# Linear attention into a routed MLP on one core: freeing the first half batches from a shared PSUM buffer, splitting one cast, and turning 512 tokens ahead of 64

## The chip, the cores and the metric

The kernel runs on one core of a Trainium2 chip. The metric is device time in microseconds of one execution, from the first to the last instruction of the program; the figure given is the median of several executions. The kernel before takes 963.41 us (median of three, 963.19 to 964.06). The profile of it is of one further execution whose recorded span is 960.4 us; all positions in time below are counted from the start of that span.

## The reference

For 8 batches and 8 heads, with 576 tokens of 64 channels each, the attention part computes with phi(x) = elu(x) + 1

```python
kv  = einsum('bhsd,bhse->bhde', phi(k), v)      # k^T v
z   = sum(phi(k), axis=2)
num = einsum('bhsd,bhde->bhse', phi(q), kv)
den = einsum('bhsd,bhd->bhs', phi(q), z)[..., None] + 1e-06
x   = (num / den)  -> transposed and reshaped to (4608, 512)
```

Then comes a mixture of 8 experts over all tokens: logits = x @ w_gate, P = exp(logits) brought to balance by eight rounds of row and column scaling, and out = sum over e of P[:, e] * (relu(x @ w1[e]) @ w2[e]), with w1[e] of 512 x 1024 and w2[e] of 1024 x 512. All inputs are fp32 in device memory; the products are computed in fp16 with fp32 sums.

## The kernel before, in words

**A planner writes the order.** Every piece of work is handed to `add` (lines 33 to 46) with its engine or engines, an assumed duration, what it depends on, and the buffers that it takes (`acq`) and uses (`use`). `_Plan.run` (lines 52 to 119) plays this forward as a list scheduler: it takes the engine that can start earliest, among what can start then the task with the lowest `prio`, and emits its instructions. So the order of the instructions on each engine is fixed when the program is built. On the chip each engine goes through its list in that order, and an instruction that waits holds up all behind it on its engine. After all tasks are added, a long string `ranks` (lines 1026 to 1163) overwrites the `prio` of tasks by their number and, with a suffix `act` or `dve`, nails a task that either engine could do to one of them. The tasks of the front and of expert 0 are in it; the tensor engine's order for experts 1 to 7 is written out by hand as a chain (lines 1011 to 1024).

**The front: 16 half batches.** `att(b, g)` (line 246) handles four heads of one batch, n = 2b + g counting the half batches from 0 to 15. It loads k, q and v (line 269; for n of 0, 1 and from 6 on by SyncE, for 2 to 5 by GpSimd), computes exp on ScalarE (line 285), and phi on VectorE in two steps (lines 298 and 301). The fp32 v is cast to fp16 into `vv` (line 315), which keeps a column of ones beside each head, so that k^T v and the sums z come from one set of 18 matmuls (line 330) into `kv_ps`, a PSUM tile [128, 2, 512] of which columns 0 to 129 of each of its two banks are used; it has one buffer. A multiplication then masks this into `kvz` (lines 341 and 343). phi(q) is transposed on TensorE (line 358) and copied out (line 362) as `qpT`. The denominators are ten small matmuls (line 373) into `den_ps`, 20 columns wide; VectorE adds 1e-6 and takes the reciprocal (lines 379 and 381, `rden`). The numerators come in three groups, of two, two and one row tile (line 397), and VectorE multiplies each with `rden` into `xn` (line 402). The five row tiles start at token pairs js = 0, 2, 4, 6 and 7, in units of 64 tokens: the last overlaps the fourth, so that tiles 0 to 3 hold tokens 0 to 511 and only the last 64 tokens come from tile 4. Each channel chunk of 128 is then transposed with five transposes (line 413) and copied with one copy of 576 columns (line 417) into `xT`, which holds all tokens channels first.

**Shared PSUM.** The tag `att` has two buffers (`aps`, line 159). Transposed q, the denominators, the numerators, the transposed x, the logits and later pieces of the experts all take one of the two in the order of the plan (pool `p_att`). For n = 0 the first two numerator groups use `ye0` and `ye1` instead (`ps_home`, line 250).

**What follows.** `layer1(0, g)` (line 560) multiplies 512 tokens with w1 of expert 0 in eight column tiles f. For g = 0 the first four are cut in two: channel chunks 0 and 1 (half batch 0 alone) first, then chunks 2 and 3, which need half batch 1 (lines 572 and 573). It waits for `xt_done` of all batches that its tokens lie in: g = 0 lies in batch 0 alone, g = 1 in batches 0 and 1. The second layer (line 809) follows in `unit_plain`, in groups of four matmuls over half of w2 each, with two PSUM buffers `ye0` and `ye1`, and an accumulator takes both halves. `x_blocks` (line 598) prepares and stores shuffled sums of `xT`, `logits` (line 425) multiplies with w_gate, and `sinkhorn` does the eight rounds. Experts 1 to 7 follow, with a form of multiplication that saves one product in eight.

**Loads at the start.** SyncE issues k, q, v of n = 0 and 1 at once. On GpSimd's queue come, in an order that the dependencies fix: w1 of expert 0 in two parts (after v of n = 0 has landed, line 522), the loads of n = 2, those of n = 3, w2 of expert 0 in two parts (line 527), and then n = 4 and 5. `kqin` and `vin` have two buffers each, so the loads of n + 2 wait until those of n are read.

**Warm-up.** 34 tasks of one or two dummy matmuls (lines 503 to 513, 47 matmuls in all) with the lowest priority are spread over the first 18 us, to keep TensorE in work until the real matmuls come.

Of the kernel before, what the change touches and what calls it, by code (L numbers as in the profile page):

```python
# [122 lines left out]
def kernel(  # L123
# [45 lines left out]
    NX = 5  # L169
    MG = 99  # L170
# [67 lines left out]
    gates = {}  # L238
    v_land, kv_id = [], []
# [6 lines left out]
    def att(b, g):  # L246
# [67 lines left out]
        def f_v(e):  # L314
            copy(e, gvv["tile"][:, :, :, 0:D], gin["v"]["tile"])
        tvv.append(fadd({"act": 1.15, "dve": 0.76}, f_v, deps=[ta, tin["v"]],
                        use=[gvv, gin["v"]], prio=pr))
# [49 lines left out]
        gden, grd, gxn = S_.grp(p_att), S_.grp(p_rden), S_.grp(p_xn)  # L367

        def f_den(_):
            gden["tile"] = aps.tile([P, 5, 2, 2], FP32, tag="att", name="den_ps")  # L370
            for i, j in enumerate(js):
                for hh in range(2):
                    nc.tensor.matmul(gden["tile"][:, i, :, hh],  # L373
                                     lhsT=gq["tile"][:, hh, j:j + 2, :].rearrange("p j w -> p (j w)"),
                                     rhs=gz["tile"][:, hh, :, D], start=True, stop=True)

        def f_rd(_):
            grd["tile"] = fp.tile([P, 5, 4], FP32, tag="rden", name="rden")
            nc.vector.tensor_scalar(out=grd["tile"], in0=gden["tile"].rearrange("p i r h -> p i (r h)"),
                                    scalar1=1e-6, scalar2=None, op0=ALU.add)  # L380
            nc.vector.reciprocal(grd["tile"], grd["tile"])
        tden = fadd(("pe", 0.26), f_den, deps=tq + tz, acq=[gden], use=[gq, gz], prio=pr)
# [6 lines left out]
        for i0, i1 in ((0, 2), (2, 4), (4, 5)):  # L389
# [16 lines left out]
            txn.append(fadd(("dve", 0.14 + 0.275 * (i1 - i0)), f_xn, deps=[t1, trd, txa], use=[gn, grd, gxn], prio=pr))  # L406
        for c2 in range(2):
            gx = S_.grp(p_att)

            def f_xt(_, c2=c2, gx=gx):  # L410
                gx["tile"] = aps.tile([P, S], FP16, tag="att", name="xt_ps")
                for i in range(5):
# [3 lines left out]
            def f_xc(e, c2=c2, gx=gx):  # L416
                copy(e, xT[:, 2 * g + c2, S * b:S * b + S], gx["tile"])
            t1 = fadd(("pe", 0.3), f_xt, deps=txn, acq=[gx], use=[gxn], prio=pr)
            xt_done[(b, 2 * g + c2)] = fadd({"act": 0.64, "dve": 0.46}, f_xc, deps=[t1], use=[gx], prio=pr)
# [5 lines left out]
    def logits(b2):  # L425
# [11 lines left out]
        t1 = lg_pe[b2] = add(("pe", 1.0), f_l, deps=[xt_done[(b, c)] for b in (2 * b2, 2 * b2 + 1) for c in range(NDT)],  # L437
# [74 lines left out]
    for i in range(34):  # L512
# [47 lines left out]
    def layer1(e, g):  # L560
        gw1, tw1, gw2, tw2 = w_t[e]
        bs = range(512 * g // S, (512 * g + 511) // S + 1)
        xd_ = [xt_done[(b, c)] for b in bs for c in range(NDT)]
# [34 lines left out]
    def x_blocks(g):  # L598
        bs = range(512 * g // S, (512 * g + 511) // S + 1)
        deps = [xt_done[(b, c)] for b in bs for c in range(NDT)]  # L600
# [420 lines left out]
    for tt in (3, 2, 1, 0):  # L1021
# [5 lines left out]
        0:-50.0024 36:8.7509 38:8.7566 40:-50.0207 42:-49.9982 43:8.7608 44:-50.0228 45:8.7578 46:-50.0192  # L1027
        47:-50.0138 49:8.7452:act 50:-49.9982 51:-50.0108 52:-50.0204:act 54:8.7572 55:-50.0216 56:8.7563
        57:-49.9985:act 58:-50.0222 59:-50.0213 61:-50.0117 62:-50.0036 63:-50.012 64:8.759 65:-50.0135
        66:-98.0291 67:-50.012 68:8.7602:dve 69:-49.9994 70:-50.0129:act 71:-50.015 73:-50.0144 75:-49.9886  # L1030
        77:-50.0129 78:-49.9988 79:-50.0186 80:8.7587 81:-50.0207 82:-50.0027 84:-50.0198 85:-49.9829
        86:-49.9985:act 88:-98.021 89:-50.015:act 90:-50.0201 91:8.7617:dve 92:-50.0195 93:-50.0219
        95:-50.0162 96:8.7575 97:-50.0201 98:-50.0186 99:8.7464 100:-98.0051 101:-50.0195 102:-50.0144:act
        103:-50.0141 104:-50.0198 106:8.7632 108:8.7575 110:-49.9844 112:-50.0216 114:-50.0006 116:8.7575
        117:-50.0132 118:-50.0006 119:-50.021 120:-50.0192 121:-49.9982 123:-50.0201:dve 124:-50.0159
        125:-50.0225:dve 127:-50.0138 128:-50.0105:dve 129:8.762 130:-50.0213 131:-98.0054 132:-50.0189
        134:-49.9787 135:-50.0207 136:-49.9859 137:-50.003 138:-50.0018 139:-50.0228 140:-50.0153
        141:-50.0093:dve 142:-49.9811 143:-50.0003:dve 144:-50.0156 146:-50.012 148:-50.0147 150:-50.0237
        151:-50.021 152:8.7593 153:-50.0204 154:-50.0192 155:-50.0156 157:-50.0003:act 158:-50.0159
        159:8.7368:dve 161:-50.0117 162:-50.0147:act 163:-50.0021 164:-50.0213 165:-50.0222 166:8.7443  # L1040
        168:-50.021 169:-50.0231 170:-50.0168 171:-50.0267 172:-50.0216 173:-50.0144 174:-50.0228
        175:-50.0228:dve 176:-50.0201 177:-49.9787:act 179:-50.0063 181:-50.006 183:-50.0144 184:-50.0189
        185:-50.0189 187:-50.0168 189:-50.0048 191:8.7584 192:-49.9802 193:-50.0225 194:-50.0255
        195:-50.0201 196:-50.0219 198:-50.0195 199:-50.0132 200:-50.0207:dve 202:-50.0249 203:-50.0144
        204:-50.0015 205:-50.0213:dve 206:-98.0237 207:-50.012 209:-50.0183 210:-50.0204 211:-50.0258
        212:-50.0288 213:-50.0189 214:-50.0237 215:-49.9808 216:-49.9856:act 217:-50.0219 218:-50.0117:dve
        219:8.7602 221:-50.0153 223:-49.9991 225:-50.0015 226:-50.0165 227:-50.0225 228:-50.0162
        229:-98.0078 230:-50.0165 232:-50.0087:dve 233:-98.0054 234:8.7512:dve 236:-50.0216 237:-98.0051:act
        238:-50.0246 239:-50.0165:dve 240:-50.0219 241:-98.0048 243:-50.027 244:-50.0195 245:-50.0135
        246:-50.0126 247:-50.0228 248:-50.0123 249:-50.0159 250:-50.018:act 251:-98.0228 252:-49.9826  # L1050
        253:-50.018 255:-50.0213 257:-50.018 259:-50.0162 260:-50.0231 261:-98.0063 262:-50.0282 263:-50.012
        264:-50.0003 266:-50.0117:dve 267:-50.0159 268:8.7464:act 270:-50.0195 271:8.7509:act 272:-98.0054
        273:-50.0168 274:-50.0162 275:-98.0246 277:-50.015 278:-50.0213 279:-50.0243 280:-50.0273
        281:-50.0174 282:-98.0231 283:-98.003 284:-50.0198:act 285:-98.0261 286:-50.0228:dve 287:-98.0048
        289:-49.9814 291:-49.9808 293:-50.0267 294:-49.9856 295:-50.0282 296:-50.0045 297:-50.0243
        298:8.7446 300:-49.9805 301:-50.0276 302:-50.0186:dve 304:-50.0204 305:-50.0123:act 306:-50.0132
        307:-98.006:act 308:-50.0207 309:-50.0219 311:-49.9784 312:-50.0192 313:-50.0189 314:-50.0123
        315:-50.021 316:-50.012 317:-49.9754 318:-50.0135 319:-50.0162 320:-49.9826:act 321:-50.0015
        322:-50.0249 323:-50.0126 325:-98.0048 327:-50.0198 329:-50.0108 330:-50.0174 331:8.7458 332:-49.985
        333:-50.0162 334:-50.0153 336:-50.0159:dve 337:-50.0171 338:-49.9793:dve 340:-98.0294 341:-98.033  # L1060
# [140 lines left out]
```

The softmax here doesn't subtract the row's maximum and nothing guards it: scores larger than these inputs give would overflow.

## Time and profile before

| what | value |
|---|---|
| time, median of 3 | 963.41 us (963.19 to 964.06) |
| span of the profiled execution | 960.4 us |
| TensorE matmul busy | 954.2 us, 8833 instructions |
| VectorE, ScalarE, GpSimd busy | 773.4, 572.4, 114.1 us |
| granted TensorE clock | 1.00 in all stretches |
| memory traffic | 121.99 MB by DMA, mean 127 GB/s, 270 to 345 GB/s in the first 120 us |

A page of the profile lists the busy time of each engine, then the span in 40 slices, the DMA queues, the chain of work that ended last, and the costliest groups of instructions. PE is the tensor engine's matmuls and PEld its weight loads, which overlap them. DVE is VectorE, ACT ScalarE, POOL GpSimd and SP SyncE. A group is named by its line in the kernel, and "out<-in" are the tiles' names. In an answer of the timeline the columns are the start, the duration and the engine; brackets at the end tell how long the engine sat idle before, and what ended that. Three things matter for reading it here: the dummy matmuls count as busy, an instruction of TensorE is shown with its latency and overlaps the next (four matmuls of 512 columns are listed with 1.03 us, but follow each other in 0.86), and the front, where the change lies, is the first 130 us.

### The profile page before, as it was taken

What the parts mean: (1) busy time and instruction counts of PE and PEld (TensorE: products, weight loads), DVE (VectorE), ACT (ScalarE), POOL (GpSimd) and SP (SyncE); (2) the same over time, 40 slices, a digit from 0 to 9 for tenths busy, and PEclk for the clock granted to TensorE, in tenths of its full rate; (3) what the DMA queues carried; (4) which work ended last, traced back from release to release, by engine and by line L of the source; (5) the groups of instructions that cost most, each with busy time, mean ns of one, the idle gap of its engine ahead of it and who ended that gap; (6) DMA issues with size and microseconds to landing.
All of it is one profiled execution on the core that took longest, in us unless ns stands there. A gap on an engine that the chain in (4) does not pass through costs nothing.

```text
span 960.4 us, 21585 instructions
## 1 busy us (share of the span) xinstructions
PE 954.2 (99%) x8833; PEld 803.7 (84%) x8833; DVE 773.4 (81%) x1527; ACT 572.4 (60%) x1034; POOL 114.1 (12%) x163
## 2 busy tenths in 40 slices
PE   9999999999999999999999999999999999999998
PEld 4666676688888888888888888888888888888886
DVE  6998889878887888878887888878887888877775
ACT  6897755855555555555555555555555555555553
POOL 4100000011111111111111100111111111111110
PEclk9999999999999999999999999999999999999999
DMA  9987962252227222452227222272226321235554
GB/s 317 345 315 259 277 195 77 44 122 78 78 77 165 78 77 78 113 130 77 78 78 164 79 78 78 81 162 74 68 71 136 93 78 74 78 100 164 166 162 114
DMA packets 46420, 121.99 MB, mean 127 GB/s; under 512 B 4208, under 2 KB 18288, under 8 KB 46320
## 3 DMA queue, kind: packets, MB, share of 16 engines
q1 hardware_dynamic: 30576, 96.22, 30.1%
q0 software_dynamic: 15344, 23.87, 12.9%
q8 instruction: 69, 1.13, 0.5%
q10 hardware_dynamic: 400, 0.52, 0.2%
q14 instruction: 31, 0.25, 0.1%
HBM read 119.69 MB, written 17.69 MB: 143 GB/s over the span
## 4 chain that ended last, share of the span: by engine, by line
PE 95%; DMA 2%; ACT 2%; DVE 0%; issue 0%; POOL 0%; ACTq 0%; DVEq 0%
PE ye L927 34%; PE hq L703 24%; PE att L703 12%; PE ye L809 7%; PE Zye L703 6%; PE Zye L927 6%; PE hq L583 3%; DMA kqin<-in_k_dram 2%; ACT e L285 1%; PE xt_ps L413 1%; PE kv_ps L330 1%; PE num_ps L397 1%; PE qt_ps L358 1%; ACT h L587 0%; PE lg_ps L432 0%; PE den_ps L373 0%
## 5 line engine op out<-in xcount | busy, mean ns | idle before, releaser
L941 DVE SCALAR_TENSOR_TENSOR acc<-ye,P_sb,acc 128x256 f32<-128x256 f32 x620 | 267.3, 479 | 128.1 <-PE ye L927 127.6
L703 PEld LDWEIGHTS <-W 128*128 128x128 f16 x2144 | 209.8, 98 | 26.8 <-issue 0.2
L927 PEld LDWEIGHTS <-S 128*128 128x128 f16 x1984 | 194.1, 98 | 22.5
L927 PE MATMUL ye<-T,S 128*128 128x256 f16 x1488 | 192.8, 273 | 0.0
L703 PEld LDWEIGHTS <-w 128*128 128x128 f16 x1608 | 157.4, 98 | 20.1 <-issue 0.7
L735 ACT ACTIVATE h<-hq 128x512 f16<-128x512 f32 x134 | 80.1, 597 | 146.2 <-PE hq L703 143.3
L951 POOL TENSOR_TENSOR acc<-acc,st 128x256 f32<-128x256 f32 x124 | 87.3, 724 | 619.9 <-ACT st L948 609.2
L927 PEld LDWEIGHTS <-h 128*128 128x128 f16 x1488 | 145.6, 98 | 16.8
L703 PE MATMUL att<-xs,W 128*128 128x256 f16 x1008 | 151.2, 273 | 0.0
L703 PE MATMUL hq<-xs,W 128*128 128x256 f16 x1008 | 151.2, 273 | 0.0
L703 PE MATMUL hq<-xs,w 128*128 128x256 f16 x1008 | 140.9, 273 | 0.3 <-DVE h L738 0.3
L732 ACT ACTIVATE h<-Zye 128x512 f16<-128x512 f32 x134 | 80.1, 598 | 42.6 <-PE Zye L703 42.6
L948 ACT ACTIVATE st<-Zye,P_sb 128x256 f32<-128x256 f32 x124 | 51.9, 470 | 78.0 <-PE Zye L927 78.0
L900 DVE TENSOR_TENSOR S<-h 128x1024 f16<-128x1024 f16 x124 | 85.4, 689 | 13.7 <-ACT h L735 13.7
L738 DVE CUSTOM_DVE_ANT_0 h<-att,s 128x512 f16<-128x512 f32 x126 | 86.7, 688 | 11.7 <-ACT s L722 11.1
L722 ACT COPY s<-hq 128x512 f32<-128x512 f32 x126 | 73.6, 584 | 36.3 <-PE hq L703 36.3
L715 ACT COPY Zye<-hq 128x512 f32<-128x512 f32 x134 | 78.0, 582 | 17.8 <-PE hq L703 17.7
L738 DVE CUSTOM_DVE_ANT_0 h<-hq,s 128x512 f16<-128x512 f32 x126 | 86.7, 688 | 0.6 <-PE hq L703 0.6
L809 PE MATMUL ye<-w,h 128*128 128x512 f16 x312 | 76.6, 379 | 0.0
L703 PE MATMUL Zye<-xs,w 128*128 128x256 f16 x504 | 75.6, 273 | 0.0
L729 ACT COPY s<-att 128x512 f32<-128x512 f32 x126 | 74.6, 592 | 0.0
L927 PE MATMUL ye<-w,h 128*128 128x256 f16 x496 | 64.3, 273 | 0.0
(109 smaller groups left out, 949.7 us busy)
## 6 DMA issues: line engine op xcount, KB each, us to landing
xs<-xd SPq DMA_DIRECT2D x63, 896.0 KB, 4.6
w<-in_moe_w_dram POOLq DMA_DIRECT2D x14, 1024.0 KB, 11.5
out_dram<-acc SPq DMA_DIRECT2D x67, 128.0 KB, 2.4
kqin<-in_k_dram SPq DMA_DIRECT2D x12, 576.0 KB, 5.2
kqin<-in_q_dram SPq DMA_DIRECT2D x12, 576.0 KB, 6.6
vin<-in_v_dram SPq DMA_DIRECT2D x12, 576.0 KB, 7.3
xd<-acc SPq DMA_DIRECT2D x5, 512.0 KB, 4.9
kqin<-in_k_dram POOLq DMA_DIRECT2D x4, 576.0 KB, 10.5
```

Source lines behind the costliest of these rows:

```text
L703: nc.tensor.matmul(dst[:, p, :], lhsT=lhs(p, c), rhs=rhs(c), start=(first and p == 0 and c == 0), stop=(c == 1), skip_group_check=True)
L715: nc.scalar.copy(out=Zt[1], in_=gX["tile"])
L722: nc.scalar.copy(out=gs2["tile"], in_=gX["tile"])
L729: nc.scalar.copy(out=gs5["tile"], in_=gR["tile"])
L732: nc.scalar.activation(out=hd(0, 0), in_=Zt[1], func=AF.Relu)
L735: nc.scalar.activation(out=hd(1, 0), in_=gX["tile"], func=AF.Relu)
L738: nc.vector._custom_dve(TENSOR_ADD_SAT, out=dst, in0=ps, in1=sb, s0=3.0e38, s1=0.0)
L809: nc.tensor.matmul(gy[tt]["tile"], lhsT=gh["tile"][:, f, ds(P * tt, P)], rhs=gw2["tile"][:, f, :], start=(f == 0), stop=(f == NFT - 1))
L900: nc.vector.tensor_tensor(out=Sx[:, i], in0=a0, in1=a1, op=op)
L927: nc.tensor.matmul(bank(g_)[:, s, :], lhsT=lhs(s, kk), rhs=rhs(kk), start=(new and s == 0 and kk == 0), stop=(kk == 3), skip_group_check=True)
L941: nc.vector.scalar_tensor_tensor(out=dst(), in0=bank(g_)[:, s, :], scalar=P_sb[:, gg, e:e + 1], in1=dst(), op0=ALU.mult, op1=ALU.add)
L951: nc.gpsimd.tensor_tensor(out=dst(), in0=dst(), in1=gst["tile"], op=ALU.add)
```

## The change

Four parts, all in `att` but the last:

1. For the first two half batches (n < ND = 2) the denominators are no longer written to a buffer of the tag `att` but to columns 256 to 275 of the first bank of `kv_ps`, which the k^T v matmuls leave unused. So they take no place in the turn of the two `att` buffers; `kv_ps` is held until `rden` has read them.
2. The cast of v of n = 1 is cut into two halves of 576 elements per partition, which can be done by ScalarE and VectorE or one after the other.
3. For n < 2 each chunk's turning covers tokens 0 to 511 alone (four transposes and a copy of 512 columns), and it depends on the first two numerator groups only. The last 64 tokens of both chunks are turned afterwards into one buffer and copied together. What needs only the first 512 tokens (`layer1` and `x_blocks` of g = 0) does not wait for this last part; g = 1 and the first logits do.
4. The string `ranks` is replaced: other priorities for nearly all tasks of the front and of expert 0, and other choices between ScalarE and VectorE. Three dummy matmul tasks of one matmul each are dropped from the end of the warm-up.

The parts' purpose is to have the first 512 tokens of both half batches in `xT` sooner, so that the expert's first matmuls can start sooner.

```diff
-        def f_v(e):
-            copy(e, gvv["tile"][:, :, :, 0:D], gin["v"]["tile"])
-        tvv.append(fadd({"act": 1.15, "dve": 0.76}, f_v, deps=[ta, tin["v"]],
-                        use=[gvv, gin["v"]], prio=pr))
+        for r0, r1 in ((0, 1), (1, 2)) if n == 1 else ((0, 2),):
+            def f_v(e, r0=r0, r1=r1):
+                copy(e, gvv["tile"][:, r0:r1, :, 0:D], gin["v"]["tile"][:, r0:r1])
+            tvv.append(fadd({"act": 1.15, "dve": 0.76} if r1 - r0 == 2 else {"act": 0.64, "dve": 0.46}, f_v,
+                            deps=[ta, tin["v"]], use=[gvv, gin["v"]], prio=pr))
...
-        gden, grd, gxn = S_.grp(p_att), S_.grp(p_rden), S_.grp(p_xn)
+        gden, grd, gxn = gkv if n < ND else S_.grp(p_att), S_.grp(p_rden), S_.grp(p_xn)
+        dent = []
 
         def f_den(_):
-            gden["tile"] = aps.tile([P, 5, 2, 2], FP32, tag="att", name="den_ps")
+            if n < ND:
+                dent.append(gkv["tile"][:, 0, 256:276].rearrange("p (i r h) -> p i r h", i=5, r=2))
+            else:
+                gden["tile"] = aps.tile([P, 5, 2, 2], FP32, tag="att", name="den_ps")
+                dent.append(gden["tile"])
...
+        ni = 4 if n < 2 else 5
         for c2 in range(2):
...
-                for i in range(5):
+                for i in range(ni):
...
-                copy(e, xT[:, 2 * g + c2, S * b:S * b + S], gx["tile"])
-            t1 = fadd(("pe", 0.3), f_xt, deps=txn, acq=[gx], use=[gxn], prio=pr)
+                w = S if ni == 5 else 512
+                copy(e, xT[:, 2 * g + c2, S * b:S * b + w], gx["tile"][:, 0:w])
+            t1 = fadd(("pe", 0.06 * ni), f_xt, deps=txn if ni == 5 else txn[0:2], acq=[gx], use=[gxn], prio=pr)
...
+        if ni == 4:
+            gx = S_.grp(p_att)
+
+            def f_xu(_):
+                gx["tile"] = aps.tile([P, 2, P], FP16, tag="att", name="xt_ps")
+                for c2 in range(2):
+                    nc.tensor.transpose(gx["tile"][:, c2, :],
+                                        gxn["tile"][:, 4, 2 * c2:2 * c2 + 2, :].rearrange("p r e -> p (r e)"), ident)
+
+            def f_xv(e):
+                copy(e, xT[:, 2 * g:2 * g + 2, S * b + 512:S * b + S], gx["tile"][:, :, 64:P])
+            t1 = fadd(("pe", 0.12), f_xu, deps=[txn[2]], acq=[gx], use=[gxn], prio=pr)
+            xt_tail.append(fadd({"act": 0.23, "dve": 0.22}, f_xv, deps=[t1], use=[gx], prio=pr))
...
-    for i in range(34):
+    for i in range(31):
...
-        xd_ = [xt_done[(b, c)] for b in bs for c in range(NDT)]
+        xd_ = [xt_done[(b, c)] for b in bs for c in range(NDT)] + (xt_tail if g == 1 else [])
...
     ranks = """
...
```

## The prediction

> **What bounds the kernel.** I read the page first, then the busy time by stretches.
>
> ```profile
> PE 954.2 (99%) x8833; PEld 803.7 (84%) x8833; DVE 773.4 (81%) x1527; ACT 572.4 (60%) x1034; POOL 114.1 (12%) x163
> PE 95%; DMA 2%; ACT 2%; DVE 0%; issue 0%; POOL 0%; ACTq 0%; DVEq 0%
> ```
>
> Columns of the stretches: from:to, length, busy us and count of PE, PEld, DVE, ACT, POOL, then clock, DMA share, GB/s.
>
> ```profile
> 9.00:17.10 8.10, 8.10 (x116) 5.46 (x115) 6.08 (x14) 6.45 (x11) 6.82 (x9) 1.00 1.17 279
> 17.10:29.10 12.00, 11.64 (x102) 6.33 (x101) 10.88 (x21) 9.39 (x14) 4.72 (x7) 1.00 1.09 339
> 29.10:66.00 36.90, 36.80 (x434) 23.00 (x434) 34.10 (x68) 31.39 (x45) 1.10 (x2) 1.00 0.99 342
> 66.00:130.00 64.00, 63.68 (x752) 40.78 (x752) 52.83 (x116) 48.03 (x80) 2.09 (x3) 1.00 0.84 253
> 130.00:950.00 820.00, 819.68 (x7377) 721.53 (x7376) 662.30 (x1295) 472.26 (x883) 97.82 (x136) 1.00 0.36 101
> ```
>
> TensorE is the bound. From 29.1 to 950 us it idles 0.10 + 0.32 + 0.32 = 0.7 us in all. No part of the change removes a real matmul, so time can only come out of the first 29 us, where "busy" deceives: 47 dummy matmuls are counted. The chain of waits says when catching up ends: up to 27.97 its pieces are loads, exp, casts and ReLU; then
>
> ```profile
> 27.97 1.05 ACT vv L229
> 29.03 0.04 issue
> 29.07 0.69 PE kv_ps L330 x18
> ```
>
> and from here TensorE's own work sets the pace. From that chain's pieces, a half batch costs TensorE 0.62 (k^T v) + 0.50 (nine transposes of q) + 0.24 (denominators) + 0.58 (numerators) + 0.56 (turning) = 2.5 us, and four matmuls of the expert 0.86. Done by 29.07: n = 0 and 1 (5.0), the first layer of g = 0 (32 matmuls, 6.9), n = 2 without four numerator matmuls and the turning (2.5 - 0.23 - 0.56 = 1.7): 13.6 us of work, so 15.5 us were lost to the start. The question is how much of that comes back.
>
> **What holds the first layer up.** The timeline around the handover:
>
> ```profile
> 16.35 0.37 PEld L373 LDWEIGHTS <-qpT 128*128 128x128 f16 x10 [0.27 <-DVE xT L231]
> 17.45 1.62 DVE L402 TENSOR_TENSOR xn<-num_ps,rden 128x512 f16<-128x512 f32 x3
> 18.96 0.72 PE L413 MATMUL xt_ps<-ident,xn 128*128 128x128 f16 x10
> 19.65 0.76 DVE L298 TENSOR_SCALAR t<-kqin 128x1152 f16<-128x1152 f32 x1 [0.58 <-DMA kqin<-in_k_dram]
> 19.71 1.16 ACT L285 ACTIVATE e<-kqin 128x1152 f16<-128x1152 f32 x1 [2.89 <-DMA kqin<-in_k_dram]
> 20.33 0.45 DVE L231 COPY xT<-xt_ps 128x576 f16<-128x576 f16 x1
> 20.78 0.62 ACT L229 COPY xT<-xt_ps 128x576 f16<-128x576 f16 x1
> ```
>
> The denominators of n = 1 wait until VectorE has emptied an `att` buffer. And x of n = 1 is turned by 19.68, yet its copies start at 20.33 and 20.78, since both engines stand idle in front of a k (of n = 2) that has not landed, with the copies queued behind. The second chunks of the first layer therefore run from about 20.8 on.
>
> [...] the DMA share is 0.99 to 1.17 from 9 to 66 us, whoever issues. [...] the clock here is 1.00 throughout[...]
>
> **The change part by part, along n = 1.** v of n = 1 is issued at 3.53 and lands 9.0 us later (DMA to landing), 12.53.
>
> Split cast: ScalarE ran it whole from 12.78 to 13.94 (1.16). Half costs 0.64 on ScalarE or 0.46 on VectorE by the plan; the trace has no half. Upper bound: 576 columns of fp16 out of PSUM took 0.64 and 0.46 (copies to xT); lower: half the whole casts, 0.58 and 0.38. I take the upper. Both halves side by side end at about 13.3: 0.6 sooner. Behind VectorE's half stand its min of q and the three `xn` of n = 0, which move back by 0.46; TensorE's transposes of q wait for that min.
>
> Denominators in spare columns: they start when `qpT` is copied instead of at 16.35. q's min ends near 14.2, transposes and copies take 0.5 + 0.6, so 15.4: 0.9 sooner. The new wait: k^T v of n = 1 waits for `rden` of n = 0 to be read (12.70 + 0.17); it ran at 14.51, so nothing is lost.
>
> VectorE then binds: after `xn` of n = 0 (1.62, ending near 15.8) come `rden` (0.49) and two `xn` of n = 1 (1.2; the third no longer counts, 0.4), so 17.5 in place of 19.07.
>
> Turning four tiles of each chunk (0.45) and the copies of 512 columns (0.41 and 0.58 by the plan, against 0.45 and 0.62 measured for 576) end near 18.6, before k of n = 2 lands at 19.6, if the new order puts them first. Before: 20.78 and 21.40. So the first layer's second half can start some 2.2 us sooner. The first eight matmuls (1.7) need n = 0 and w1 (issued 8.54, landing 6.3 later, 14.9) and fill the gaps of 16.5 to 18.6.
>
> What is added: two tail copies, 0.22 each by the plan, against four copies shortened by 0.04: +0.3 us on VectorE and ScalarE, which had 1.1 and 2.6 us idle from 17.1 to 29.1: hidden. The turning stays at 40 transposes. Three dummy matmuls less are 0.6 us of filling, no saving in itself.
>
> **How much survives.** Not all of 2.2, for the loads don't move: their order on GpSimd is fixed by dependencies, and the DMA engines are full. n = 3's v lands at 14.74 + 12.3 = 27.0. w2 is the later gate, of which the second part, issued at 17.79, answers
>
> ```profile
> DMA to landing us min/median/max: 14.4/14.4/14.4
> ```
>
> so 32.2; the first lands at 15.46 + 14.0 = 29.5. Before 32.2 TensorE can at best do four half batches (10.0), the first layer of g = 0 (6.9) and two groups on the first part of w2 (1.7, there being two `ye` buffers): 18.6. Layer 1 of g = 1 needs x of n = 3: 27.0 + cast 0.76 + k^T v 0.62 + mask 0.43 + denominators 0.24 + `rden` 0.49 + `xn` 1.6 + turning 0.6 + copy 0.45 = 32.2, too late to help. Before, TensorE had done 13.6 + 3.1 = 16.7 by 32.2. The cap is 1.9 us. The turning of n = 3 (0.56) can hardly be in time by the same sum, which leaves 1.3 to 1.4. After 32.2 there is always work (second layers, first layer of g = 1), so what is won then stays. 963.4 - 1.4 = 962.0.
>
> **Rivals.**
>
> All of it is won (chance 0.32): the cap of 1.9 is reached, and the new order also takes out part of the 0.7 us idle after 29.1. For it: that idle is there, and the handover alone has 2.2. Against: n = 3's turning, and VectorE at 10.9 of 12.0 us. 963.4 - 2.4 = 961.0, down to 960.7 with all.
>
> The transfers hide it (0.08): the first layer ends earlier, but TensorE then waits for n = 3 and w2 as long as it gained. For it: full DMA. Against: at 29.07 the cast of v (n = 3, landed 27.0, begun 27.81) waited for ScalarE's ReLUs, which come earlier now. 963.3.
>
> The new order costs more than the start gives (0.14), slower: all priorities of the front are new, and from 29 to 66 us VectorE (34.1 of 36.9), ScalarE (31.4) and DMA are nearly full, so a copy placed behind a load that comes late stops TensorE, as at 19.65, for about 1.1 us. Four such stops against 1.4: 966. Against: the order of before has almost none, so the planner's durations are good.
>
> **How the numbers follow.** The main case, gain 0.7 to 1.9, has 0.46; it and the hidden transfers are within 0.2% (1.93 us): same 0.54. All won: faster 0.32. Slower 0.14. The range takes in main and all won, and the cast's bounds (0.1 us), and stops at 960.6 and 964.6, with about 0.05 left out below and 0.12 above.
>
> **What would show it.** Right: the second-chunk matmuls of line 583 start near 18.6; no wait of line 373 on an `att` buffer for n = 0 and 1; the copies of n = 1 ahead of k of n = 2; some idle or dummy time between 26 and 32 us; w2 still landing near 29.5 and 32.2; the stretch 130 to 950 as long as before. Wrong: loads that land earlier (then more is won), or TensorE idle by more than 1 us after 33 us (then it is the order).

## The result, and the profile after

The changed kernel takes 967.40 us (median of six executions, 967.19 to 969.51), the kernel before 963.30 us beside it (six, 962.64 to 964.49). The ratio is 1.0045, 95% interval 1.0032 to 1.0058: 4.1 us slower. The recorded span went from 960.4 to 965.6 us; the profile of before is of an execution of 962.2 us, 1.1 below the median, so its span is shorter than a typical one. The forecast was 962.0, with a range up to 964.6.

The page of the changed kernel has the same busy time of TensorE as before (954.2 then, 953.9 now), yet the chain that ended last is less TensorE's: loads have 4% of it (2% before) and VectorE 4% (0%):

```profile
PE 953.9 (99%) x8830; PEld 803.4 (83%) x8830; DVE 773.3 (80%) x1529; ACT 572.3 (59%) x1034; POOL 114.7 (12%) x163
PE 89%; DMA 4%; DVE 4%; ACT 1%; issue 0%; SPq 0%; POOL 0%; ACTq 0%; DVEq 0%
```

The busy time by stretches, changed kernel, columns as in the prediction:

```profile
9.00:17.10 8.10, 8.10 (x115) 5.37 (x113) 6.20 (x14) 6.02 (x10) 6.85 (x9) 1.00 1.17 278
17.10:29.10 12.00, 10.91 (x101) 6.18 (x99) 11.24 (x24) 8.88 (x13) 5.41 (x7) 1.00 1.09 340
29.10:66.00 36.90, 36.90 (x424) 22.86 (x422) 32.69 (x64) 30.47 (x46) 0.85 (x2) 1.00 0.99 343
66.00:130.00 64.00, 59.38 (x699) 37.62 (x696) 50.40 (x109) 47.99 (x76) 2.38 (x3) 1.00 0.82 246
130.00:950.00 820.00, 819.50 (x7403) 720.69 (x7401) 662.51 (x1297) 471.33 (x882) 97.62 (x136) 1.00 0.35 101
```

TensorE's idle time is length minus busy. From 17.1 to 130 us it is now 1.09 + 0 + 4.62 = 5.7; before it was 0.36 + 0.10 + 0.32 = 0.8. The difference, 4.9 us, is nearly the whole 5.2 by which the span grew, and 4.3 of it lie between 66 and 130 us, far from the edited half batches. (The 0.7 at the start may be chance: the kernel before, profiled once more, idled 1.08 there.) From 130 us on TensorE's busy time is the same.

Which waits these are, TensorE's waits in the changed kernel say (total us, times, longest):

```profile
PE num_ps L405 <- ACT qpT L230: 2.2, 1, 2.2
PE num_ps L405 <- ACT xT L230: 1.4, 1, 1.4
PE hq L607 <- DVE xT L232: 0.8, 1, 0.8
PE xt_ps L422 <- ACT qpT L230: 0.5, 1, 0.5
PE hq L607 <- ACT h L611: 0.4, 1, 0.4
```

Numerators wait twice for a copy on ScalarE. The chain of waits of the changed kernel, from 84 us on, shows what that copy was held up by (start, us, what):

```profile
84.66 0.34 SPq L660
85.05 0.43 SPq L630
85.52 0.53 SPq L631
86.16 0.76 SPq L271
86.97 9.74 DMA kqin<-in_q_dram
96.73 1.16 ACT e L287
97.89 0.59 ACT qpT L230
98.52 0.39 PE num_ps L405 x4
...
101.55 7.81 DMA kqin<-in_q_dram
109.38 1.16 ACT e L287
110.55 0.49 ACT h L611
111.03 0.54 ACT xT L230
111.61 0.28 PE num_ps L405 x2
```

The first three pieces are the stores of `x_blocks` for g = 2 (lines 660, 630 and 631), 512 + 128 + 256 = 896 KB; then come the loads of n = 14. q needs 9.74 us to land, k 9.1. On ScalarE's list the two exps of n = 14 stand ahead of copies of `qpT` and `xT` whose transposes are done by 95.5. The list is fixed, so ScalarE idles until k lands at 95.3, does the exps, and only then the copies; TensorE stands from 96.4 to 98.5. The same comes again with q of n = 15, at 111. ScalarE's first exp of n = 14, in the kernel before and then in the changed one:

```profile
98.97 1.16 ACT L285 ACTIVATE e<-kqin 128x1152 f16<-128x1152 f32 x1
95.34 1.16 ACT L287 ACTIVATE e<-kqin 128x1152 f16<-128x1152 f32 x1 [2.24 <-DMA kqin<-in_k_dram]
```

In the kernel before, k of n = 14 is issued at 91.83, lands 5.2 us later, at 97.0, and nobody waits for it. So the load is late only for the place that the new list gives it: in absolute time it lands 1.7 us sooner than before.

What the list counted on can be read from the planner's own times, which come out when the program is built. They count 1.55 us of transfer and 2.6 us of latency for a load, and let transfers wait for each other. Near the start they fit the chip: for the kernel before they have k of n = 2 landing at 19.3, v of n = 3 at 27.0 and w2 at 29.7 and 32.3; the profile has 19.6, 27.0, 29.5 and 32.2. For the changed kernel they have k of n = 14 landing 5.6 us after its issue, where the chip took 9.1. The planner takes waiting transfers by priority, and stores have the lowest: those of g = 2, issued 1.4 us ahead of this k, start in the plan only after all three loads of n = 14. On the chip SyncE issues them ahead of these loads, from 84.66 us on, and the load behind them is 3.5 us longer in flight than planned.

At the start nothing was won either. The changed kernel's timeline around the handover to layer 1 (start, us, engine, instruction; idle time before it in brackets):

```profile
12.54 1.25 ACT L230 CAST vv<-vin 128x576 f16<-128x576 f32 x2
16.60 0.41 PE L381 MATMUL kv_ps<-kvz,qpT 128*128 128x2 f16 x10
17.73 1.62 DVE L410 TENSOR_TENSOR xn<-num_ps,rden 128x256 f16<-128x256 f32 x3
18.87 0.27 PE L437 MATMUL xt_ps<-ident,xn 128*128 128x128 f16 x2
19.50 0.61 PE L422 MATMUL xt_ps<-ident,xn 128*128 128x128 f16 x8
19.83 0.76 DVE L300 TENSOR_SCALAR t<-kqin 128x1152 f16<-128x1152 f32 x1 [0.48 <-DMA kqin<-in_k_dram]
20.51 0.74 DVE L232 COPY xT<-xt_ps 128x512 f16<-128x512 f16 x2
```

Both halves of the cast went to ScalarE; the denominators of n = 1 run at 16.60, not earlier than 16.41 before; the last 64 tokens are turned (18.87) ahead of the first 512 (19.50); and the copies of x of n = 1 still stand behind k of n = 2, both on VectorE, at 20.51. The second chunks of layer 1 wait 0.77 us for the first of them and start at 21.31; the forecast had 18.6.

### The profile page after: what moved, and what is told of

The parts are those of the page before. It is cut to its first block, busy times and chain, and to the rows that moved or that the text cites. A ratio compares the mean times of both kernels' runs of the same rounds, so it can differ in the third digit from the quotient of the medians.

```text
span 965.6 us, 21581 instructions
## 1 busy us (share of the span) xinstructions
PE 953.9 (99%) x8830; PEld 803.4 (83%) x8830; DVE 773.3 (80%) x1529; ACT 572.3 (59%) x1034; POOL 114.7 (12%) x163
## 3 DMA queue, kind: packets, MB, share of 16 engines
q1 hardware_dynamic: 30576, 96.22, 29.8%
## 4 chain that ended last, share of the span: by engine, by line
PE 89%; DMA 4%; DVE 4%; ACT 1%; issue 0%; SPq 0%; POOL 0%; ACTq 0%; DVEq 0%
PE ye L951 33%; PE hq L727 24%; PE att L727 12%; PE Zye L727 6%; PE Zye L951 6%; PE ye L833 5%; DMA kqin<-in_k_dram 2%; PE hq L607 2%; DMA kqin<-in_q_dram 2%; DVE h L762 1%; ACT e L287 1%; DVE t L300 1%; PE num_ps L405 1%; PE kv_ps L333 1%; PE qt_ps L361 0%
## 5 line engine op out<-in xcount | busy, mean ns | idle before, releaser
L951 PE MATMUL ye<-w,S 128*128 128x256 f16 x496 | 64.3, 273 | 0.0
```

Of the source, the lines that this page charges most:

```text
L951: nc.tensor.matmul(bank(g_)[:, s, :], lhsT=lhs(s, kk), rhs=rhs(kk), start=(new and s == 0 and kk == 0), stop=(kk == 3), skip_group_check=True)
```

## The experiments

All kernels below keep every computation. The numbers of `ranks` and the planner's run are replaced in them by the list of tasks in the order in which they are emitted, so that single places can be moved. In the diffs a line is a stretch of one engine's list: `ek14` is the exp of k of n = 14, `cast14` the cast of v, `tk`/`mk` the first and second step of phi(k) (the same with q), `qc`/`xc` a copy of transposed q or x, `xn` a normalisation, `relu3.4` the ReLU f = 4 of chunk g = 3, `L1.5` the layer-1 matmuls number 5 in the list, `kv` k^T v, `st2` and `raw2` the stores of `x_blocks` for g = 2. Runs of one group were taken on one chip, with the kernel before beside them. The ratio is an estimate of its own from the single runs, not the quotient of the two medians; the two differ by up to 0.0005.

| group | kernel | median us | before beside it | ratio, 95% interval |
|---|---|---|---|---|
| 1 | b_parts | 964.59 | 963.83 | 1.0007 (0.9999 to 1.0016) |
| 1 | c_order | 966.51 | 963.83 | 1.0031 (1.0019 to 1.0042) |
| 1 | a_fifo | 965.87 | 963.83 | 1.0021 (1.0014 to 1.0029) |
| 1 | d_main_first | 965.42 | 963.83 | 1.0020 (1.0009 to 1.0031) |
| 2 | g_loads_first | 964.61 | 964.15 | 1.0001 (0.9993 to 1.0009) |
| 2 | a_fifo2 | 965.81 | 964.15 | 1.0019 (1.0012 to 1.0025) |
| 2 | d2_relu_first | 964.89 | 964.15 | 1.0006 (0.9995 to 1.0016) |
| 2 | e_before_start | 964.88 | 964.15 | 1.0006 (0.9997 to 1.0016) |
| 3 | before_again | 962.72 (one run) | 963.80 | |
| 3 | c_loads_first | 964.23 | 963.80 | 1.0002 (0.9994 to 1.0010) |
| 3 | g2_start | 965.76 | 963.80 | 1.0018 (1.0010 to 1.0025) |
| 3 | e3_casts_first | 964.33 | 963.80 | 1.0001 (0.9991 to 1.0010) |
| 4 | d3_cast_first | 964.65 | 963.98 | 1.0004 (0.9996 to 1.0012) |
| 4 | d5_filled | 964.37 | 963.98 | 1.0005 (0.9997 to 1.0013) |
| 4 | e4_two_casts | 963.85 | 963.98 | 1.0002 (0.9993 to 1.0011) |

### The parts without the order, the order without the parts

```diff
 b_parts: denominators in the spare columns, cast in halves, 512 + 64 tokens
-    order of the change
+    order of before, the new small tasks put beside those they were split from
 c_order: one cast, denominators in att, 576 tokens in one copy
-    order of before
+    order of the change
```

> Parts 1 to 3 of the change with the order of before, written out task by task; the new pieces are put in where they hold up nothing (both halves of the cast one after the other on ScalarE, the tail of n = 0 after its first 512 tokens, the tail of n = 1 after the first layer of g = 0), and the three last dummy matmuls dropped. Theory 'the order costs': as before, 963.3, within 962.3 to 963.8, since the copies of n = 1 still stand behind k of n = 2. Rival 'the parts cost' (the longer hold of kv_ps, the split copies, the additional buffer turns): 966 to 967.5.

> The kernel before, none of the parts 1 to 3, with the order of after written out task by task (the pieces that do not exist there left out, the cast of v of n = 1 whole, all 34 dummy tasks). Theory 'the order costs': 967.4, within 966.3 to 968.5. Rival 'the parts cost': 963 to 964.5.

The order alone costs 0.31%, some 3.0 us; the parts alone cost 0.07%, an interval that holds zero. In the order-only kernel TensorE stops in the same two places, for less long; its timeline:

```profile
97.70 0.39 PE L397 MATMUL num_ps<-kvz,qpT 128*128 128x128 f16 x4 [1.18 <-ACT qpT L229]
110.22 0.28 PE L397 MATMUL num_ps<-kvz,qpT 128*128 128x128 f16 x2 [0.78 <-ACT xT L229]
```

So it is the order in the main: 0.31% and 0.07% make up 0.38% of the 0.45%, and the rest is within the intervals. The next question was which feature of it: where the exps stand, or why the loads are late.

### Exps moved behind what TensorE needs

```diff
 ScalarE, changed kernel -> a_fifo -> a_fifo2
- ek10 relu2.1 eq10 qc8 relu2.2 ...  ek14 eq14 qc11 xc9 relu3.4 ...  eq15 relu4.2 xc12
+ relu2.1 ek10 qc8 eq10 relu2.2 ...  qc11 xc9 ek14 eq14 relu3.4 ...  relu4.2 xc12 eq15
+ relu2.1 ek10 qc8 relu2.2 eq10 ...  qc11 xc9 ek14 relu3.4 eq14 ...  relu4.2 xc12 eq15
```

> The kernel after with seven places changed in ScalarE's order alone: exps of loads that land late (k and q of n = 10, k and q of n = 14, q of n = 15) are put behind the ReLU and the copies out of PSUM that the profile after shows TensorE waiting for. Theory 'order on ScalarE' (TensorE's 4.6 us idle between 66 and 130 come from an exp at the head of ScalarE's queue that waits for its load, with those copies behind it): the stops of 2.2 and 1.4 us at 98 and 111 us and most of the 0.9 us at 68 to 69 go, about 3.5 us, so 963.9 with 963.3 to 965. Rival 'the loads are too late' (TensorE would run out of work there whatever ScalarE does first, since the loads of n = 13 to 15 land late): the idle time only moves, 966.5 to 967.5.

> The kernel with the seven places on ScalarE moved, and two more: the exp of q of n = 10 also behind the ReLU f = 2 of g = 2, and the exp of q of n = 14 behind the ReLU f = 4 of g = 3, so that the two ReLUs that TensorE waited for (0.80 at 69.7 and 1.58 at 99.4) stand ahead of exps. Theory one (what remains of the loss at 66 to 130 us is ScalarE's order around late loads): the two waits go, TensorE's idle time there falls from 2.95 to some 1, and the time is 964 to 964.6. Theory two (the delay is only handed on, to the turning of q or to VectorE's numerators of the same n): another wait of 1 us or more in 99 to 115, and the time stays within 0.4 of 965.9.

The first gave back about 2 of the 4 us, less than expected: 965.87, between the ranges of its two theories. The two long waits are gone, but TensorE now waits for ReLUs queued behind those same exps. Its timeline:

```profile
69.70 1.02 PE L607 MATMUL hq<-xT,w 128*128 128x512 f16 x4 [0.80 <-ACT h L611]
99.36 0.81 PE L607 MATMUL hq<-xT,w 128*128 128x512 f16 x3 [1.58 <-ACT h L611]
```

The second takes away these two; idle time from 66 to 130 us falls from 2.95 to 1.97 us, but waits of 0.66 for `qpT` at 101.2, 0.53 for a ReLU at 97.6 and 0.47 for `xT` at 70.1 remain, and the time is the same within the interval. Theory two of its expectation, a delay handed on, comes nearer, though none of the new waits reaches the 1 us that it named. (In these two kernels alone the time is 2.1 us longer than the recorded span, in all others 1.8; so 0.3 us of what is left lies outside the span and is not explained.) ScalarE's list thus holds about half of the cost.

### Two stores behind three loads

```diff
 SyncE, in g_loads_first (from the changed kernel) and c_loads_first (from c_order)
- ldk13 ldq13 ldv13 st2 raw2 ldk14 ldq14 ldv14
+ ldk13 ldq13 ldv13 ldk14 ldq14 ldv14 st2 raw2
```

> The changed kernel; only the two stores of x_blocks for g = 2 are put behind the three loads of n = 14 on SyncE, which in the changed kernel stand behind them. Theory one (the exps of n = 14 stop TensorE because its loads lie behind the stores and the loads of n = 13 and land 9 to 10 us after their issue): k of n = 14 lands near 91 to 93 instead of 95.3, the 2.2 us idle at 98.5 is gone or under 0.5, and the time falls by 1.5 to 2.2 us, to some 965.3 to 966. Theory two (landing is set by all that is in flight, not by what stands ahead): k lands within 1 us of 95.3, the stop stays above 1.5, and the time stays near 967.4.

> The structure of before with the changed kernel's order (which cost 0.31% alone), and the two stores of x_blocks for g = 2 put behind the loads of n = 14 on SyncE. Theory one (the cost of the new order is those loads being late for the exps put early): 964.0 to 964.8, most of the 2.9 us back, no wait above 0.6 at 95 to 112. Theory two (the order costs in many places and the stores only hid it in the other kernel): 965.3 or more.

The two stores are three transfers, lines 660, 630 and 631. This one move, with every other engine's list untouched, brings both kernels back to the time of before: 1.0001 and 1.0002, from 1.0045 and 1.0031. Theory one holds, and the first kernel gained more than it said: 964.61, for a forecast of 965.3 to 966. The stop at 111 us is down to 0.2 us too; the loads of n = 15 are issued 1.8 us sooner there (98.96 for 100.75). The stretch from 66 to 130 us and ScalarE's timeline, both of g_loads_first:

```profile
66.00:130.00 64.00, 62.93 (x728) 39.89 (x726) 52.81 (x116) 49.23 (x78) 2.37 (x3) 1.00 0.86 256
```

```profile
93.41 2.22 ACT L287 ACTIVATE e<-kqin 128x1152 f16<-128x1152 f32 x2
95.65 0.69 ACT L230 COPY qpT<-qt_ps 128x640 f16<-128x640 f16 x1
96.24 0.65 ACT L230 COPY xT<-xt_ps 128x576 f16<-128x576 f16 x1
```

Idle time there is 1.07 instead of 4.62, and the exps run with no wait. Issue to landing of k of n = 14, first in the changed kernel, then in this one:

```profile
DMA to landing us min/median/max: 9.1/9.1/9.1
```

```profile
DMA to landing us min/median/max: 6.9/6.9/6.9
```

The issue moved by only 0.4 us (86.16 to 85.77), the landing by 2.6 (95.3 to 92.7). So here it is for the most part not SyncE's waiting for the stores' input that delayed the load, but the time in flight: at the mean 365 GB/s that the view of the DMA traffic shows for 84 to 96 us of the changed kernel, 896 KB take 2.5 us (an estimate). In the other pair it is half and half: from c_order to c_loads_first the issue moved from 86.41 to 85.40 and the time in flight from 8.0 to 6.9 us. So the delay does not simply follow the bytes ahead, and what sets its size was not tried apart.

### The copies of x ahead of the late k

The forecast had a condition, the copies of n = 1 ahead of k of n = 2, which the change did not meet. Two kernels meet it, one with the parts and one without:

```diff
 d_main_first, from b_parts
 ScalarE  - ek2 xc1a eq2 relu0.0      + xc1a ek2 eq2 relu0.0
 VectorE  - xn1c tk2 xc1b             + xc1b xn1c tk2
 TensorE  den1 ahead of the tail; num1c behind L1.4; L1.0 to L1.2 beside the turning of x1
 d2_relu_first, from d_main_first
 ScalarE  - ek2 eq2 relu0.0 relu0.1   + ek2 relu0.0 relu0.1 eq2
 VectorE  - xn1c tk2                  + tk2 xn1c
 TensorE  - L1.2, turning of x1       + turning of x1, L1.2
 e_before_start, from the kernel before
 ScalarE  - ek2 xc1a eq2 relu0.0 relu0.1   + xc1a ek2 relu0.0 relu0.1 eq2
 VectorE  - tk2 xc1b                       + xc1b tk2
```

> b_parts (parts 1 to 3, order of before) with what the parts are for carried through in the order of the start alone: denominators of n = 1 ahead, the first three cut tasks of layer 1 ahead of the turning of n = 1, its copies ahead of exp and phi of n = 2 on both engines, and the numerators of the last 64 tokens of n = 1 behind. From 25 us on the order is that of before. Theory 'the start can give 1.3 to 1.9 us, and it is kept': 961.4 to 962.0. Rival 'the start gives nothing since the loads hide it': 963.0 to 963.5.

> The three parts with the order of before, the copies of x of n = 1 ahead of the exp of k of n = 2, as in the kernel that was slower than forecast, but now also: layer 1 of chunk 2 behind the turning of the first 512 tokens, the last 64 normalised behind VectorE's 1/(1+exp) of k of n = 2, and the first two ReLUs of g = 0 ahead of the exp of q of n = 2. Theory one (the start gain exists, and ReLUs behind exps took it): the 1.21 us wait for h at 23.7 goes, no idle stretch of TensorE above 0.7 lies in 17 to 29, and the time is 961.5 to 962.7. Theory two (the loads take back what the start gives, whatever the order): the idle time comes back as a wait for v or weights in 24 to 33, and the time is 963.5 to 964.6.

> The kernel before, unchanged in its parts; only ScalarE's and VectorE's order at 18 to 24 us is changed: both copies of the first 512 turned tokens of n = 1 ahead of the exp of k of n = 2 and its 1/(1+exp), and the first two ReLUs of g = 0 ahead of the exp of q of n = 2. Theory one (what was to be won at the start hung on these places and not on the parts): faster than before by 0.5 to 1.2 us, 962.3 to 963.3, with layer 1 of g = 0 chunk 1 at 19.5 to 20. Theory two (the start is not worth anything because the loads of w2 and v at 27 to 32 gate the end of it): 963.4 to 964.2.

All three missed what they hoped for: none is faster than before, and d_main_first is slower by 0.20%. In the first, layer 1 starts sooner but runs dry, since its sums need PSUM buffers that only ReLUs free, and the ReLUs stood behind both exps of n = 2. TensorE's timeline:

```profile
23.66 1.02 PE L607 MATMUL hq<-xT,w 128*128 128x512 f16 x4 [1.21 <-ACT h L611]
25.31 0.69 PE L333 MATMUL kv_ps<-vv,t 64*128 64x130 f16 x18 [0.62 <-DVE vv L232]
```

With two ReLUs ahead (d2_relu_first) the wait moves on: the exp of q is later, VectorE's product for q with it, and the cast of v of n = 2 stands behind that product. TensorE's timeline, and then its busy time by stretches, with the granted clock as the third number from the right:

```profile
25.22 1.16 PE L333 MATMUL kv_ps<-vv,t 64*128 64x130 f16 x18 [2.09 <-DVE vv L232]
26.82 1.79 PE L607 MATMUL hq<-xT,w 128*128 128x512 f16 x4
```

```profile
22.00:24.00 2.00, 1.02 (x4) 0.38 (x4) 1.40 (x3) 2.00 (x5) 0.11 (x1) 1.00 1.04 394
26.00:27.00 1.00, 1.00 (x14) 0.77 (x9) 0.43 (x1) 1.00 (x3) 0.18 (x1) 0.50 1.25 224
```

After the idle stretch came a further loss: the clock was 0.50 for some 3.4 us (25.0 to 28.4), and four matmuls took 1.79 us in it, for 1.03 after it. As an estimate, half of the 3.2 us that TensorE was busy in that time, 1.6 us, were lost to it in that run, which left the question open whether a start gain survives.

e_before_start shows a smaller wait of the same kind (1.64 at 25.15), and then this at 73 us, TensorE's and VectorE's timeline:

```profile
73.22 0.28 PE L397 MATMUL num_ps<-kvz,qpT 128*128 128x128 f16 x2 [1.27 <-DVE xn L402]
```

```profile
71.81 0.76 DVE L298 TENSOR_SCALAR t<-kqin 128x1152 f16<-128x1152 f32 x1 [1.52 <-DMA kqin<-in_k_dram]
72.48 0.68 DVE L402 TENSOR_TENSOR xn<-num_ps,rden 128x512 f16<-128x512 f32 x1
```

A normalisation that was ready waits behind a k (n = 11) that is not there. It is the mechanism of the result again, on VectorE: a ready instruction behind one whose load has not landed.

### Every late place taken away

```diff
 e3_casts_first, from e_before_start
 VectorE  - mk2 tq2 mq2 cast2         + mk2 tq2 cast2 mq2
          - tk11 xn7a rd8             + xn7a rd8 tk11
 e4_two_casts, from e3_casts_first
 ScalarE  - relu0.6 cast3 relu0.7     + relu0.6 relu0.7
 VectorE  - tq3 rd2                   + tq3 cast3 rd2
 g2_start, from g_loads_first: as d2 and e3 at 19 to 25 us
 d3_cast_first, from d2_relu_first
 VectorE  - mk2 tq2 mq2 cast2         + mk2 tq2 cast2 mq2
 d5_filled, from d3_cast_first: cast3 as in e4, and
 TensorE  - kv2 qt2a L1.9             + L1.9 kv2 qt2a
```

> The kernel before, its instructions and their order unchanged, profiled on the chip of the other runs of this call, so that the landing of its loads can be compared with theirs. If loads land later here than in the first profile, k of n = 2 lands at 20.2 to 20.5 instead of 19.65, and the first matmuls of layer 1 on x of n = 1 start that much later; if the landing is a matter of the changed kernels, it lands near 19.65 again.

> The changed kernel with the two stores behind the loads of n = 14, and at 19 to 25 us also: the copies of x of n = 1 ahead of the exp of k of n = 2 (one of them on ScalarE), two ReLUs of g = 0 ahead of the exp of q of n = 2, and the cast of v of n = 2 ahead of VectorE's product for q. Theory one (the start can give some 1.5 us, and the places behind loads ate it): the 1.76 us wait at 22 goes, no other above 0.7 comes before 30, and the time is 1 to 1.6 us under the kernel with the stores alone, 963.0 to 963.6. Theory two (loads of n = 2 gate k^T v of n = 2 near 24 to 25, and until then TensorE has nothing but layer 1 of g = 0): idle of 1 us or more comes back just ahead of that k^T v, and the time is within 0.5 of 964.6.

> The kernel before with its order changed at 18 to 24 us (copies of x of n = 1 ahead of the exp of k of n = 2, two ReLUs ahead of the exp of q), and now also the cast of v of n = 2 ahead of VectorE's product for q, and VectorE's 1/(1+exp) of k of n = 11 behind the numerators of n = 7 and the reciprocal of n = 8, which it held up by 1.27 us at 73. Theory one (the places at late loads cost the gain): 0.5 to 1.2 us below before, the wait at 73 gone and that at 25 under 1.0. Theory two (the loads take the gain back): within 0.4 of before or slower, and a new wait behind a load comes between 30 and 112 us.

> The kernel with the three parts, before's order, the first 512 tokens' copies and two ReLUs ahead (which waited 2.09 us for the cast of v of n = 2, after which TensorE's clock was 0.50 from 25.0 to 28.4, some 1.6 us lost), and now the cast of v of n = 2 ahead of VectorE's product for q. Theory one (cast's place and the clock took the gain): k^T v of n = 2 starts near 24.2 instead of 25.2, the clock stays 1.00, and the time is 962.3 to 963.3. Theory two (loads gate the end of the start, so nothing survives): the clock stays 1.00 too, but the wait comes back between 26 and 31 us and the time is 963.6 to 964.5.

> The same, with the cast of v of n = 3 moved from ScalarE to VectorE, ahead of the denominators' reciprocal of n = 2, and four layer-1 matmuls (f = 5 of g = 0) ahead of k^T v of n = 2, into the 1.1 us in which TensorE waits for v. Theory one: no idle stretch of 0.5 us between 17 and 30 us, 0.3 to 0.8 below the kernel with the cast alone. Theory two (v of n = 3 and w2, landing at 27 to 28 and 29.5 to 30.3, are the gate): idle time of 0.5 us or more moves to just ahead of k^T v of n = 3 or of the first second-layer matmul, which starts within 0.4 us of 30.6 as before, and the time is within 0.3 of the kernel with the cast alone.

> The kernel before with the copies of n = 1, two ReLUs and the cast of v of n = 2 ahead, and now the cast of v of n = 3 on VectorE. None of the three parts is in it. If the parts bring something once the start is not held up by places behind loads, the kernel with them is faster than this one by 0.4 us or more; if they bring nothing, both are within 0.4. Against before: 0.3 to 1.0 faster if ScalarE's queue of ReLUs and casts at 26 to 30 us was what kept the last gain, within 0.3 if the loads are.

before_again is the kernel before, written as a list; it is there for the landing times, which wander between executions: k of n = 2 landed at 20.0 in it and at 19.6 in the first profile. g2_start was a bad test: it put the cast ahead of the product that the q transposes need, and in the changed kernel's order these stand ahead of k^T v, so TensorE idled 2.88 us (`PE qt_ps L361 <- DVE t L303: 2.9, 1, 2.9`) and its clock was 0.50 from 25 to 28 us.

The other four are clean, with the clock at 1.00 from 17 to 66 us and no wait over 0.7 us from 17 to 130 us except one of 1.10 in d5_filled and one of 0.83 in d3_cast_first, both for a ReLU. None is faster than before: e3 1.0001, d3 1.0004, d5 1.0005, e4 1.0002; the intervals leave room for a gain of at most 0.09%, so the 1.4 us of the forecast (0.15%) are ruled out for these orders. By the times theory two holds. The table gives, from issue plus landing and from TensorE's timeline, when data landed and when the work on it began (us):

| run | v of n = 2 lands | its k^T v | v of n = 3 lands | its k^T v | w2, first part, lands | second layer starts |
|---|---|---|---|---|---|---|
| before | 22.7 | 24.22 | 27.0 | 29.07 | 29.5 | 30.21 |
| before_again | 23.0 | 24.61 | 27.5 | 29.47 | 29.8 | 30.61 |
| the change | 22.8 | 24.18 | 27.3 | 29.24 | 29.7 | 30.39 |
| e3_casts_first | 23.4 | 24.19 | 27.7 | 29.74 | 30.1 | 30.88 |
| d3_cast_first | 23.2 | 24.08 | 27.6 | 29.61 | 30.1 | 30.74 |
| d5_filled | 23.4 | 24.29 | 27.9 | 29.58 | 30.3 | 31.29 |
| e4_two_casts | 22.7 | 23.85 | 27.2 | 29.33 | 29.5 | 30.77 |

k^T v of n = 2 starts 0.9 us after its v in d3, for 1.5 before, so 0.6 us were won there. By k^T v of n = 3 they are gone: that starts 1.7 to 2.1 us after its v in every row, and the second layer 0.6 to 0.8 after w2 in the first five and 1.0 and 1.3 in the last two. Between the two, TensorE waits for ReLUs. d5_filled, TensorE's timeline:

```profile
24.29 0.69 PE L333 MATMUL kv_ps<-vv,t 64*128 64x130 f16 x18 [0.18 <-DVE vv L232]
26.74 1.02 PE L607 MATMUL hq<-xT,w 128*128 128x512 f16 x4 [1.10 <-ACT h L611]
```

The filled matmuls are done before 24.3, so what filled the time after it is missing there: the wait has moved, but to layer 1's ReLUs. In none of these four runs does TensorE wait for v of n = 3 or for w2 themselves, so that the loads gate the start, which theory two says, is not shown. What the loads do set is a bound: the second layer cannot start before w2, and it starts 0.6 to 0.8 us after it already. Whether some order uses that room stays open.

With nothing large in their way, the kernels with the three parts (d3, d5) take 964.65 and 964.37, those without (e3, e4) 964.33 and 963.85, intervals overlapping. They differ in TensorE's list at the start too, so this is no clean pair; but no run shows a gain from the parts.

## Why the prediction was wrong

**The bound.** Right: TensorE's work is the same, and from 130 to 950 us it is busy for 819.5 of 820 as before.

**Split cast, 0.6 sooner.** Mis-sized, for the halves did not run side by side. Both are on ScalarE, 12.54 to 13.79, so it ends 0.15 sooner than before. And k^T v of n = 1 did not wait for it: it follows the transposes of q, at 14.32 for 14.51.

**Denominators 0.9 sooner, then `xn` to 17.5.** They came at 16.60. Part 1 takes the denominators out of the turn of the two `att` buffers, but part 3 puts a new piece in, the last 64 tokens: those of n = 0 are turned at 14.95, and the second group of transposed q, which before ran with the first from 13.91 on, comes at 15.28, its copy ending at 16.29. Where the order puts them first (d2_relu_first) they run at 15.61, about as forecast, but the numerators come at 16.44, because they need one of the two `att` buffers, and both hold x of n = 0 (the second chunk and the last 64 tokens) until its copies are out. ScalarE's and TensorE's timeline there:

```profile
15.81 0.86 ACT L230 COPY xT<-xt_ps 128x512 f16<-128x512 f16 x2 [0.35 <-PE xt_ps L422]
```

```profile
15.61 0.41 PE L381 MATMUL kv_ps<-kvz,qpT 128*128 128x2 f16 x10
16.44 0.66 PE L405 MATMUL num_ps<-kvz,qpT 128*128 128x128 f16 x8
```

The first of the two copies takes 0.58, so it ends at 16.39. The wait was handed from the denominators to the numerators. The forecast followed the denominators out of the buffers and not what took their place.

**Copies of n = 1 by 18.6, "if the new order puts them first".** It does not: 20.51, behind k of n = 2 landing at 19.8, where before had 20.33 and 20.78. The forecast named the condition and did not follow the order out of the ranks. And where the condition is met (d_main_first), ReLUs behind the exps take its place.

**The cap of 1.9, of which 1.4 is taken.** Mis-sized: it measures nothing, within 0.1%, with every late place mended. It counted how much work TensorE could have done by 32.2 us, and left out that layer 1 of g = 0 has four PSUM buffers, freed by ReLUs on the engine that also does the exps; in the runs above TensorE waits for these ReLUs at 22 to 28 us, by up to 1.2 us at a time.

**"After 32.2 there is always work, so what is won then stays."** This is the step that made the forecast wrong in sign. It put the cost of the new order after the start at nothing. There is always work on TensorE's list, but not always work whose inputs are there: loads of the front still land up to 109 us, and the order decides what stands behind them. The changed kernel lost 4.3 us between 66 and 130 us.

**The rivals.** The third is what happened, with its mechanism as written: a copy behind a load that comes late. Four stops were counted on at 1.1 us; after 66 us there were two large ones, 2.16 and 1.35, and two of about 0.5, and no gain at the start to set against them: 967.4 for 966. What is called a stop of TensorE "as at 19.65", from which the 1.1 came, was a delay of the copies; TensorE itself idled only 0.36 us from 17.1 to 29.1 there. The rival was given 0.14 because the order of before had no such stops, "so the planner's durations are good". For the order of before they are, loads included. For the changed one they are not where stores are issued just ahead of loads: 5.6 us planned for k of n = 14, 9.1 on the chip. The order of before could not show this: k of n = 13 takes 8.9 us there too, but it is issued at 81.9 and its exp runs at 92.2, and the stores of g = 2 come behind k and q of n = 14. The new order put three store transfers ahead and the exps early. The second rival is right in that nothing is won at the start; that transfers hide it is not shown, since the waits there are for ReLUs.

**What would show it.** "TensorE idle by more than 1 us after 33 us (then it is the order)" was the reading that applied, and the runs agree. Three of the forecast's sums are off by their rounding (15.3 for 15.4, 960.8 for 960.7, 966.4 for 966), which changes nothing.

## What to carry to other kernels

- Where a list scheduler fixes each engine's order, compare the planned landing of each load with the landing in the profile, and do it again for each new order: here the plan was right to 0.4 us at the start in the order of before and 3.5 us too short for k of n = 14 in the new one, where it let loads pass stores issued ahead of them (2.2 of the 3.5 us went when these stores were moved). Work placed behind a load on ScalarE or VectorE is a bet on that landing, and when it is lost, TensorE pays for copies whose inputs were ready: 2.16 and 1.35 us in the changed kernel, at 96.4 and 110.3.
- A store issued just ahead of a load can delay it: k of n = 14 was 2.2 and 1.1 us longer in flight behind 896 KB of stores. Moving them behind the three loads was worth all of the 0.45% here, within an interval of 0.1%.
- A gain at the start can be gone by the next load, cast or ReLU: in d3_cast_first k^T v of n = 2 came 0.6 us sooner after its v than before, and by k^T v of n = 3 none of it was left. Follow a gain to the next load before counting it.

## What was not expected of the hardware

- **Loads behind stores.** With 896 KB of stores issued just ahead by the same engine, a load of 576 KB (k of n = 14) took 9.1 us from issue to landing, for 6.9 without, and in the other pair of kernels 8.0 for 6.9.
- **The clock after a short idle stretch.** In d2_relu_first TensorE's last matmuls before the wait end at 23.13, and the clock is 0.50 from about 25.0 to 28.4; in g2_start they end at 22.1, and the clock is 0.50 from about 24.9 to 28.3. In the first, TensorE had been fully idle for under 2 us before 25.0, and busy for 1.02 of the 2 us from 22 on; in the changed kernel the clock stayed at 1.00 through and after the stop of 2.16 us at 96.4. What tells the two apart was not tried.
- **Landing times wander.** k of n = 2 landed at 19.6 and 20.0 us in two profiles of the same program, and between 19.6 and 20.5 over all kernels, with the same loads issued ahead of it. Between those two profiles TensorE's idle time from 17.1 to 29.1 us differs by 0.7 us (0.36 before, 1.08 in before_again), with nothing changed in the kernel. A difference at the start between two profiles that is smaller than that says nothing by itself.
